# A kernel of attention, a dense block and routed experts: its opening made with one round trip for all key maxima, its routing's scatters spread over three blocks

## The chip, the cores and the metric

The kernel runs on one core of a Trainium2 chip. TensorE (PE) multiplies matrices into PSUM, VectorE (DVE) and ScalarE (ACT) work element by element, GpSimd (POOL) too, and it issues the indirect DMAs; SyncE (SP) issues the other DMAs. Each engine takes its instructions in the order written, so an instruction that waits holds up all that stand behind it on its engine. The metric is device time of one execution in microseconds (us), the median of several runs.

## The reference

Inputs q, k, v have the shape (8, 8, 576, 64): batch, heads, sequence, head size. What is computed, shortened:

```python
q_s = exp(q - max(q, -1)); q_s /= sum(q_s, -1) + 1e-9         # softmax over the head's 64
k_s = exp(k - max(k, 2));  k_s /= sum(k_s, 2) + 1e-9          # softmax over the sequence
kv  = einsum('bhsd,bhse->bhde', k_s, v)
x   = einsum('bhsd,bhde->bhse', q_s, kv)                      # -> 4608 tokens x 512
h   = x @ w_in;  x = (h * clip(h + 3, 0, 6) / 6) @ w_out      # weights stored as float64
e   = argmax(x @ w_gate)                                      # one of 8 experts per token
out = gate * sigmoid(x @ w_output_gate)[e] * (relu(x @ w1[e]) @ w2[e])
```

## The kernel before

The 4608 tokens go through attention and the dense block in 16 groups of 288 (`g`), two for each batch entry `b`. A group's dense block is a loop of 16 blocks (`fb`): four k-steps of `h_mm` (x by a 128-wide slice of w_in, into the PSUM tile `hps`), `h_ev` (ACT's ReLU and DVE's product), and `x2_mm` three blocks later (into four PSUM tiles `acc`). Between these stand the attention of the next group (`att_steps`) and the routing of the group before (`route1` to `route4`). After the groups come tiles of 256 tokens for the experts, each with a gather of its tokens, 8 steps of `h2_mm` and of `y_mm`, and a scatter of its rows. All orders are written out by hand: the text of the program is the order on each engine.

The opening is what stands ahead of block 0 of group 0. Eight DMAs bring k and v of batch entry 0 in four pairs of heads (`hp`, 96 partitions x 768 numbers each), two bring q for group 0 (`a`). For each pair `k_max` reduces six rows to one (DVE), `k_max_tr` transposes it (PE, into `kmps`), `k_max_diag` takes the maximum along the row and puts it on a diagonal (DVE, `mc` and `dg`), `k_max_row` multiplies by ones so that each partition holds the maxima (PE, `kmrow`). That is one round trip between DVE and PE for each pair, four in all, with the rest of the attention between them: `k_sub` (DVE), `k_exp` (ACT), `v_pad` (ACT copies v beside a column of ones), `kv_mm` (PE), `kv_ev` (DVE makes the reciprocal, ACT scales into `kvbd`), `q_a`, `q_exp`, `q_b` (softmax of q), `q_tr` (PE transposes, ACT copies to `qT`), `x0_mm` (PE, ACT copies to `xhi`). `pe_warm` issues matmuls whose result nobody reads.

The weights w_in and w_out come as float64. `dec_act` (L186, L188, ACT) and `dec_vec` (L192, L194, DVE) turn a tile of them into float32 in place; in group 0, `decode_step` does so for the next tiles, between the blocks. In groups 1 and 2, `split` (L200 on ACT, L202 on DVE or POOL) makes a high and a low part of each weight tile for the later groups. Its result goes into a buffer of a pool of 33 (`wsl`), so ACT's cast may have to wait until the tile that sat there has had its last reader.

`route4` of the group before stands in block 11 of each group from 1 on. It ends with three indirect DMAs on POOL (L530), which scatter 96 entries each into the table `tbl` in DRAM. They write one tensor, so the second waits until the first has landed, and the third for the second. Behind them in POOL's queue stand that block's `gl` (L407, low part of the activations) and, in group 2, its half of `split` (L202).

Of the kernel before, what the change touches and what calls it, by code (L numbers as in the profile page):

```python
# [8 lines left out]
F32 = mybir.dt.float32  # L9
# [11 lines left out]
def kernel(  # L21
# [227 lines left out]
    def v_pad(b, hp):  # L249
        t = big([PR, R, 2 * D + 1], F32, "io", 7, "vt")  # L250
        nc.gpsimd.memset(t[:, :, 2 * D:], 1.0)
        nc.scalar.copy(t[:, :, 0:2 * D].rearrange("p r (h d) -> p r h d", h=2), vt[b, hp].rearrange("p h r d -> p r h d"))
        vt[b, hp] = t

    def load_q(g, a):
        b, hf = divmod(g, 2)
        src = lambda h: q[b, 4 * a + h].rearrange("(p r) d -> p r d", r=R)[:, hf * RH:(hf + 1) * RH, :]
        if g < 2:
            t = wsl.tile([PR, 4, RH, D], F32, tag="w", name="qraw")
            nc.sync.dma_start(  # L260
                out=t.rearrange("p h r d -> p h (r d)"),
                in_=q[b, 4 * a:4 * a + 4].rearrange("h (p r) d -> p h (r d)", r=R)[:, :, hf * RH * D:(hf + 1) * RH * D])
            qt[g, a] = t.rearrange("p h r d -> p r h d")
            return
# [58 lines left out]
    def kv_ev(b, hp):  # L323
        ps = kvps.pop((b, hp))
        rs = sb.tile([128, 1], F32, tag="rs", name="rs")
        nc.vector.tensor_scalar(out=rs, in0=ps[:, 2 * D:2 * D + 1], scalar1=1e-9, scalar2=None, op0=ALU.add)
        nc.vector.reciprocal(out=rs, in_=rs)
        for h in range(2):
            a = slice(h * D, (h + 1) * D)
            nc.scalar.activation(out=kvbd[a, hp, a], in_=ps[a, a], func=ACTF.Copy, scale=rs[a])  # L330

    def q_a(g, a):
        t = qt[g, a]
# [5 lines left out]
        eng.tensor_tensor(out=qt[g, a], in0=t, in1=m.unsqueeze(3).to_broadcast([PR, RH, 4, D]), op=ALU.subtract)  # L339

    def q_exp(g, a):
        t = qt[g, a].rearrange("p r h d -> p (r h d)")
        nc.scalar.activation(out=t, in_=t, func=ACTF.Exp)

    def q_b(g, a):
        t = qt[g, a]
        m = sb.tile([PR, RH, 4], F32, tag="qs", name="qs")
        nc.vector.tensor_reduce(out=m, in_=t, axis=AX.X, op=ALU.add)
        nc.vector.tensor_scalar(out=m, in0=m, scalar1=1e-9, scalar2=None, op0=ALU.add)
        nc.vector.reciprocal(out=m, in_=m)  # L350
        eng = nc.gpsimd if g < 2 else nc.vector
        eng.tensor_tensor(out=t, in0=t, in1=m.unsqueeze(3).to_broadcast([PR, RH, 4, D]), op=ALU.mult)

    qT = {}

    def q_tr(g, hp):
        t = qt[g, hp // 2]
        ps = pat.tile([128, 512], F32, tag="a", name="qtps")
        for r in range(RH):
            c = (hp % 2) * 2  # L360
            nc.tensor.transpose(ps[:, r * PR:(r + 1) * PR], t[:, r, c:c + 2, :].rearrange("p h d -> p (h d)"), ident[0:PR, 0:PR])
        s = big([128, G], F32, "qT", 1, "qT")
# [7 lines left out]
    def x0_mm(g, hp):  # L370
        if hp == 0:
            xhi[g] = big([128, KD, G], F32R if g else F32, "xh", 2, "xhi")
            if g:
                xlo[g] = big([128, KD, G], F32R, "xl", 2, "xlo")
        ps = pat.tile([128, 512], F32, tag="a", name="x0ps")
# [133 lines left out]
    def route4(g):  # L509
# [358 lines left out]
    with tc.manual_schedule():  # L868
        constants()
        route_constants()  # L870
        fill_constants()
        load_k(0, 0)
        load_q(0, 0)
        load_k(0, 1)
        load_v(0, 0)
        load_k(0, 2)
        load_q(0, 1)
        load_k(0, 3)
        load_v(0, 1)
# [6 lines left out]
        pe_warm(10)  # L886
        k_max(0, 0)
        k_max_tr(0, 0)
        q_a(0, 0)
        q_exp(0, 0)  # L890
        k_max_diag(0, 0)
        k_max_row(0, 0)
        k_max(0, 1)
        k_max_tr(0, 1)
        k_sub(0, 0)
        k_exp(0, 0)
        v_pad(0, 0)
        k_max_diag(0, 1)
        k_max_row(0, 1)
        q_b(0, 0)  # L900
        k_max(0, 2)
        k_sub(0, 1)
        k_max_tr(0, 2)
        k_exp(0, 1)
        v_pad(0, 1)
        kv_mm(0, 0)
        k_max_diag(0, 2)
        k_max_row(0, 2)
        kv_ev(0, 0)
        q_a(0, 1)  # L910
        k_max(0, 3)
        k_sub(0, 2)
        q_tr(0, 0)
        k_max_tr(0, 3)
        kv_mm(0, 1)
        k_exp(0, 2)
        v_pad(0, 2)
        q_exp(0, 1)
        k_max_diag(0, 3)
        k_max_row(0, 3)  # L920
        kv_ev(0, 1)
        k_sub(0, 3)
        x0_mm(0, 0)
        q_tr(0, 1)
# [12 lines left out]
        dec_vec(1)
        x0_mm(0, 2)
        q_tr(0, 3)
        x0_mm(0, 3)  # L940
        dec_act(2)
        dec_act(3)
        for g in range(NG):
            st = att_steps(g + 1)
            for fb in range(NF):
# [29 lines left out]
                if g > 0:  # L975
# [164 lines left out]
```

## Time and profile before

| | |
|---|---|
| median of 3 runs | 1468.23 us (1467.95 to 1469.39) |
| the profiled execution's own time | 1460.46 us |
| its span | 1458.7 us |
| PE busy | 1408.2 us, 97% |
| DVE, ACT, POOL busy | 59%, 46%, 33% |
| mean granted clock of TensorE | 0.986 of full speed |

A row of the timeline gives the start from the span's beginning, the duration, engine, line, operation, the tile written and the tile read, and in brackets the idle time of the engine before it with what ended it. A granted clock of 1.00 is TensorE's level of 2.4 GHz, 0.50 that of 1.2 GHz. PE's busy time comes from modelled ends, so a PE that is always busy may still run at half its clock.

### The profile page before, as it was taken

How to read it: one execution, taken by the hardware profiler on the slowest of the kernel's cores; microseconds unless marked ns; L12 is line 12 of the kernel's file. 1: busy time of each engine (PE TensorE's matmuls, PEld its weight loads, DVE VectorE, ACT ScalarE, POOL GpSimd, SP SyncE). 2: the span in 40 equal slices, each digit the busy share in tenths (PEclk: the TensorE clock that was granted, in tenths of full speed). 3: DMA queues.
4: the chain of work that ended last, by engine and by line, in shares of the span. 5: the costliest groups of instructions: out<-in, count | busy, mean ns of one | idle time of the engine just before them, and what ended most of it. 6: DMA issues, size and time to landing. Idle time of an engine off the chain costs nothing. (4 is left out here: it accounts for less than half of the span.)

```text
span 1458.7 us, 27464 instructions
## 1 busy us (share of the span) xinstructions
PE 1408.2 (97%) x9668; PEld 1322.5 (91%) x9668; DVE 860.7 (59%) x2151; ACT 670.4 (46%) x1479; POOL 486.8 (33%) x544
## 2 busy tenths in 40 slices
PE   6999998999999999999999999999999999999997
PEld 5788998999999999999999999999888898998996
DVE  6976364545634735545554473637868676767743
ACT  5854353433433433343343343334645565655643
POOL 1113363222222222222322222344444545455431
PEclk7999999999999999999999999999999999999999
DMA  9912021121220202212122020034767677877774
GB/s 292 322 39 58 21 51 27 44 50 25 56 53 18 53 14 58 52 24 58 26 50 50 17 58 17 2 99 137 235 195 217 210 227 224 246 221 245 231 253 147
DMA packets 195749, 161.17 MB, mean 110 GB/s; under 512 B 116828, under 2 KB 147793, under 8 KB 195602
## 3 DMA queue, kind: packets, MB, share of 16 engines
q1 hardware_dynamic: 186114, 139.51, 33.5%
q0 software_dynamic: 9488, 19.82, 4.2%
q8 instruction: 78, 1.28, 0.4%
q14 instruction: 69, 0.57, 0.1%
HBM read 139.03 MB, written 20.49 MB: 109 GB/s over the span
## 5 line engine op out<-in xcount | busy, mean ns | idle before, releaser
L390 PE MATMUL hps<-xhi,w 128*128 128x288 f32 x1920 | 427.9, 298 | 0.0
L418 PE MATMUL acc<-gh,w 128*128 128x288 f32 x1800 | 410.7, 306 | 0.0
L407 POOL TENSOR_TENSOR gl<-r,gh 128x288 fp32r<-128x288 f32 x225 | 182.0, 810 | 540.9 <-ACT gh L406 510.0
L390 PEld LDWEIGHTS hps<-xhi,w 128*128 128x128 f32 x1920 | 321.4, 188 | 1.5
L418 PEld LDWEIGHTS acc<-gh,w 128*128 128x128 f32 x1800 | 301.7, 189 | 3.4
L390 PE MATMUL hps<-xlo,w 128*128 128x288 f32 x960 | 283.2, 295 | 0.0
L400 DVE SCALAR_TENSOR_TENSOR r<-r,hps 128x288 f32<-128x288 f32 x225 | 101.4, 451 | 306.8 <-ACT r L399 298.9
L418 PE MATMUL acc<-gl,w 128*128 128x288 f32 x900 | 265.7, 295 | 0.0
L399 ACT ACTIVATE r<-hps,half 128x288 f32<-128x288 f32 x225 | 112.6, 500 | 263.2 <-PE hps L390 258.8
L821 PE MATMUL h2ps<-x2h,wb 128*128 128x256 f32 x1088 | 216.9, 282 | 1.6 <-issue 1.3
L772 POOL DMA_INDIRECT gx<-x2d,idx x148 | 163.8, 1106 | 140.0 <-issue 126.2
L737 DVE TENSOR_TENSOR wb<-rawb,wb 128x512 fp32r<-128x512 f32 x296 | 191.6, 688 | 13.7 <-ACT wb L736 6.1
L839 PE MATMUL y<-wb,hh 128*128 128x512 f32 x592 | 190.6, 403 | 0.8 <-issue 0.8
L821 PEld LDWEIGHTS h2ps<-x2h,wb 128*128 128x128 f32 x1088 | 176.6, 189 | 9.3 <-issue 2.4
L390 PEld LDWEIGHTS hps<-xlo,w 128*128 128x128 f32 x960 | 181.0, 189 | 0.8
L418 PEld LDWEIGHTS acc<-gl,w 128*128 128x128 f32 x900 | 170.8, 190 | 2.9
L736 ACT CAST wb<-rawb 128x512 fp32r<-128x512 f32 x296 | 168.3, 619 | 2.6 <-DMA rawb<-in_moe_w_dram 2.3
L406 ACT CAST gh<-r 128x288 fp32r<-128x288 f32 x225 | 97.4, 433 | 140.4 <-DVE r L400 139.9
L821 PE MATMUL h2ps<-x2l,wb 128*128 128x256 f32 x544 | 152.8, 281 | 8.0 <-DVE x2l L802 6.9
L825 ACT ACTIVATE hh<-h2ps 128x256 fp32r<-128x256 f32 (+1 forms) x160 | 58.9, 369 | 176.1 <-PE h2ps L821 95.7
L826 DVE SCALAR_TENSOR_TENSOR hl<-h2ps,hh 128x256 fp32r<-128x256 f32 (+1 forms) x160 | 62.9, 395 | 116.1 <-issue 58.0
L839 PE MATMUL y<-wb,hl 128*128 128x512 f32 x296 | 117.9, 398 | 0.3 <-issue 0.3
(201 smaller groups left out, 1810.5 us busy)
## 6 DMA issues: line engine op xcount, KB each, us to landing
rawb<-in_moe_w_dram SPq DMA_DIRECT2D x296, 256.0 KB
x2d<-xrow SPq DMA_DIRECT2D x60, 144.0 KB
raw<-in_moe_w_in_dram SPq DMA_DIRECT2D x16, 512.0 KB
raw<-in_moe_w_out_dram SPq DMA_DIRECT2D x16, 512.0 KB
qt<-in_q_dram SPq DMA_DIRECT2D x112, 72.0 KB
kt<-in_k_dram SPq DMA_DIRECT2D x56, 144.0 KB
vt<-in_v_dram SPq DMA_DIRECT2D x56, 144.0 KB
w1h<-in_moe_w_dram SPq DMA_DIRECT2D x24, 256.0 KB
```

Source lines behind the costliest of these rows:

```text
L390: nc.tensor.matmul(ps[:, 0:G], weight("in", fb, part, kk), x[:, kk, :], start=(n == 0), stop=(n == len(parts) * KD - 1))
L399: nc.scalar.activation(out=r, in_=ps[:, 0:G], func=ACTF.Relu, bias=half, scale=1.0 / 6.0)
L400: nc.vector.scalar_tensor_tensor(out=r, in0=r, scalar=1.0, in1=ps[:, 0:G], op0=ALU.min, op1=ALU.mult)
L406: nc.scalar.copy(gh, r)
L407: nc.gpsimd.tensor_tensor(out=gl, in0=r, in1=gh.bitcast(F32), op=ALU.subtract)
L418: nc.tensor.matmul(acc[g][eb][:, 0:G], weight("out", fb, part, eb), x, start=(fb == 0 and n == 0), stop=(fb == NF - 1 and n == len(parts) ...
L736: nc.scalar.copy(w[:, 0, :], raw)
L737: nc.vector.tensor_tensor(out=w[:, 1, :], in0=raw, in1=w[:, 0, :].bitcast(F32), op=ALU.subtract)
L772: nc.gpsimd.indirect_dma_start(out=st["gx"][:, kk, :], out_offset=None, in_=x2q, in_offset=bass.IndirectOffsetOnAxis(ap=st["idx"][:, kk:kk ...
L821: nc.tensor.matmul(ps[:, 0:m], w[:, wl, c], x[:, kk, 0:m], start=(kk == 0 and n == 0), stop=(kk == KD - 1 and n == 2))
L826: nc.vector.scalar_tensor_tensor(out=hl[:, 0:m], in0=ps[:, 0:m], scalar=0.0, in1=hh[:, 0:m].bitcast(F32), op0=ALU.max, op1=ALU.subtract)
L839: nc.tensor.matmul(st["y"][t2], hx[:, c], w[:, wl, :], start=(fb == 0 and n == 0), stop=(fb == NF2 - 1 and n == 2))
```

## The change

Two things, in the diff below. First, the opening. SP issues the four k tiles first, then q and v. `first_max` takes the maximum of a pair's six rows with three DVE operations in place of one reduction, and all four transposes go into one PSUM tile. `first_row` then makes one reduction, one diagonal of 512 columns, and one matmul of 512 columns. `pe_warm` stands between these steps: 8, four times 2, 4, and 6. The subtraction for q moves to POOL for both halves and works in place, as does `k_sub`; the copy of v for the last pair moves to POOL; `kv_ev` scales the first two pairs on DVE. `kv_mm` of the four pairs stands ahead of all `q_tr` and `x0_mm`; `dec_act(1)` stands behind the last `x0_mm`. Second, `route4` no longer issues its scatters; a new function `scatter` issues one in each of blocks 11, 12 and 13 (for the last group: in steps 3, 4 and 5 of expert tile 4).

```diff
+    def first_max(hp):
+        if hp == 0:
+            first["st"] = big([128, 2, 512], F32, "xh", 2, "first")
+            first["tr"] = pat.tile([128, 512], F32, tag="a", name="kmps0")
+        t = kt[0, hp]
+        m3 = big([PR, 3, 2, D], F32, "xs", 3, "km3")
+        m = first["st"][0:PR, 0, hp * 128:(hp + 1) * 128]
+        mv = m.rearrange("p (h d) -> p h d", h=2)
+        nc.vector.tensor_tensor(out=m3, in0=t[:, 0:3], in1=t[:, 3:6], op=ALU.max)
+        nc.vector.tensor_tensor(out=mv, in0=m3[:, 0], in1=m3[:, 1], op=ALU.max)
+        nc.vector.tensor_tensor(out=mv, in0=mv, in1=m3[:, 2], op=ALU.max)
+        nc.tensor.transpose(first["tr"][:, hp * PR:(hp + 1) * PR], m, ident[0:PR, 0:PR])
+    def first_row():
...
+        nc.vector.tensor_reduce(out=mc, in_=first.pop("tr")[:, 0:4 * PR].rearrange("p (i s) -> p i s", s=PR),
+                                axis=AX.X, op=ALU.max)
+        dg = first["st"][:, 1, :]
+        nc.vector.tensor_tensor(out=dg.rearrange("p (i d) -> p i d", i=4),
...
+        pe_warm(4)
+        ps = pat.tile([128, 512], F32, tag="a", name="kmrow0")
+        nc.tensor.matmul(ps[0:PR, :], onesf, dg, start=True, stop=True)
...
+    def first_qmax(a):
+        m = sb.tile([PR, RH, 4], F32, tag="qm", name="qm")
+        nc.vector.tensor_reduce(out=m, in_=qt[0, a], axis=AX.X, op=ALU.max)
+        nc.gpsimd.tensor_tensor(out=qt[0, a], in0=qt[0, a], in1=m.unsqueeze(3).to_broadcast([PR, RH, 4, D]),
+                                op=ALU.subtract)
...
-        for r in range(RH):
-            nc.gpsimd.indirect_dma_start(
-                out=tv, out_offset=bass.IndirectOffsetOnAxis(ap=posi[:, r:r + 1], axis=0),
-                in_=ent[:, r, :], in_offset=None)
+        rt[g] = tv, posi, ent
+
+    def scatter(g, r):
+        tv, posi, ent = rt[g]
+        nc.gpsimd.indirect_dma_start(
+            out=tv, out_offset=bass.IndirectOffsetOnAxis(ap=posi[:, r:r + 1], axis=0),
+            in_=ent[:, r, :], in_offset=None)
...
                     if fb == 11:
                         route4(g - 1)
+                    if 11 <= fb < 11 + RH:
+                        scatter(g - 1, fb - 11)
```

The opening's order on DVE, from the first key tile on, before: one pair's maximum (L275), maximum along the row (L288), diagonal (L292) and subtraction (L306), and then the next pair's.

```order
L275 TENSOR_REDUCE km<-kraw 96x128
L335 TENSOR_REDUCE qm<-qraw 96x12
L339 TENSOR_TENSOR qt<-qraw,qm 96x768
L288 TENSOR_REDUCE mc<-kmps 128x1
L292 TENSOR_SCALAR dg<-ident,mc 128x128
L275 TENSOR_REDUCE km<-kraw 96x128
L306 TENSOR_TENSOR kt<-kraw,kmrow 96x768
L288 TENSOR_REDUCE mc<-kmps 128x1
L292 TENSOR_SCALAR dg<-ident,mc 128x128
L348 TENSOR_REDUCE qs<-qt 96x12
```

The same engine and place now, from the last pair's maximum on (three operations, L281 to L283; `first` holds the maxima and later the diagonals).

```order
L281 TENSOR_TENSOR km_228<-kraw 96x384
L282 TENSOR_TENSOR first<-km_228 96x128
L283 TENSOR_TENSOR first<-first,km_228 96x128
L288 TENSOR_REDUCE mc_236<-kmps_203 128x4
L291 TENSOR_TENSOR first<-ident,mc_236 128x512
L302 TENSOR_REDUCE qm<-qraw 96x12
L340 TENSOR_TENSOR kraw<-kraw,kmrow_244 96x6x2x64 x2
L302 TENSOR_REDUCE qm<-qraw 96x12
L340 TENSOR_TENSOR kraw<-kraw,kmrow_244 96x6x2x64 x2
L390 TENSOR_REDUCE qs<-qraw 96x12
```

The four subtractions now stand behind the last pair's arrival, and nothing but q's maxima stands between them.

POOL in group 2 around the scatters of group 1, before (`w` is the low half that `split` makes, `gl` that of the activations).

```order
L202 TENSOR_TENSOR w<-raw,w 128x512
L530 DMA tbl<-ent,posi 43264x4 x3
L407 TENSOR_TENSOR gl<-r,gh 128x288
L202 TENSOR_TENSOR w<-raw,w 128x512
L407 TENSOR_TENSOR gl<-r,gh 128x288
L202 TENSOR_TENSOR w<-raw,w 128x512
```

The same place now.

```order
L577 DMA tbl<-ent,posi 43264x4
L451 TENSOR_TENSOR gl<-r,gh 128x288
L202 TENSOR_TENSOR w<-raw,w 128x512
L577 DMA tbl<-ent,posi 43264x4
L451 TENSOR_TENSOR gl<-r,gh 128x288
L202 TENSOR_TENSOR w<-raw,w 128x512
L577 DMA tbl<-ent,posi 43264x4
L451 TENSOR_TENSOR gl<-r,gh 128x288
```

One block's `gl` and `w` now stand between each scatter and the next.

## Rows read from the trace of the kernel before

**Rows 1.** The page: busy time of PE, and a group of DVE operations.

```profile
PE 1408.2 (97%) x9668; PEld 1322.5 (91%) x9668; DVE 860.7 (59%) x2151; ACT 670.4 (46%) x1479; POOL 486.8 (33%) x544
...
L737 DVE TENSOR_TENSOR wb<-rawb,wb 128x512 fp32r<-128x512 f32 x296 | 191.6, 688 | 13.7 <-ACT wb L736 6.1
```

**Rows 2.** Waits of PE over the whole run: waiter, awaited, total us, times, longest.

```profile
PE x0ps L376 <- ACT qT L363: 7.0, 4, 4.5
```

**Rows 3.** Windows of the opening: busy us by engine, then granted clock, DMA share, GB/s.

```profile
0.00:5.00 5.00, 3.45 (x16) 3.45 (x17) 2.65 (x22) 1.28 (x1) 1.75 (x13) 1.00 0.63 156
5.00:10.00 5.00, 1.88 (x10) 1.21 (x9) 4.85 (x7) 0.84 (x1) 0.00 (x0) 0.87 1.09 252
25.00:30.00 5.00, 5.00 (x26) 4.71 (x26) 1.92 (x5) 3.86 (x8) 1.47 (x1) 0.58 1.06 323
30.00:35.00 5.00, 2.89 (x16) 2.13 (x15) 1.71 (x4) 3.60 (x9) 0.00 (x0) 1.00 1.07 375
```

**Rows 4.** Timeline of the opening and of the first blocks, PE, DVE and ACT.

```profile
1.55 4.29 PE L220 MATMUL warm<-ident 128*128 128x128 f32 x20 [1.55 <-POOL ident L94]
4.20 1.47 DVE L275 TENSOR_REDUCE km<-kraw 96x128 f32<-96x768 f32 x1 [1.09 <-DMA kraw<-in_k_dram]
34.28 0.40 ACT L377 COPY xhi<-x0ps 128x288 f32<-128x288 f32 x1 [0.84 <-PE x0ps L376]
39.57 0.49 ACT L399 ACTIVATE g<-hps,half 128x288 f32<-128x288 f32 x1
40.60 2.22 PE L390 MATMUL hps<-xhi,raw 128*128 128x288 f32 x8 [2.47 <-DVE g L400]
43.62 2.22 PE L390 MATMUL hps<-xhi,raw 128*128 128x288 f32 x8 [0.81 <-DVE g L400]
```

**Rows 5.** Groups of instructions from 0 to 34 us: busy us, mean ns, idle before.

```profile
L319 PE MATMUL kvps<-vt,kt 96*128 96x129 f32 x48 | 10.6, 405 | 0.0
L306 DVE TENSOR_TENSOR kt<-kraw,kmrow 96x768 f32<-96x768 f32 x4 | 3.8, 942 | 0.1
L311 ACT ACTIVATE kt<-kt 96x768 f32<-96x768 f32 x4 | 3.4, 843 | 6.3 <-DVE kt L306 6.3
L352 POOL TENSOR_TENSOR qt<-qt,qs 96x768 f32<-96x768 f32 x2 | 2.9, 1469 | 11.8 <-DVE qs L350 11.8
L348 DVE TENSOR_REDUCE qs<-qt 96x12 f32<-96x768 f32 x2 | 1.9, 942 | 0.0
L363 ACT COPY qT<-qtps 128x288 f32<-128x288 f32 x4 | 1.6, 400 | 1.8 <-PE qtps L361 1.8
L330 ACT ACTIVATE kvbd<-kvps,rs 64x64 f32<-64x64 f32 x8 | 2.5, 306 | 1.7 <-PE kmrow L298 1.7
L288 DVE TENSOR_REDUCE mc<-kmps 128x1 f32<-128x96 f32 x4 | 1.0, 246 | 0.0
L186 ACT ACTIVATE raw<-raw,floorb 128x512 int32<-128x512 uint16 x2 | 1.5, 757 | 0.0
L188 ACT ACTIVATE raw<-raw 128x512 f32<-128x512 f32 x2 | 1.3, 644 | 0.0
```

**Rows 6.** Timeline of PE, one pair of keys later in the run.

```profile
119.50 1.50 PE L319 MATMUL kvps<-vt,kt 96*128 96x129 f32 x12
```

**Rows 7.** Timeline of DVE, an operation of the decode, while POOL runs one.

```profile
51.12 1.85 DVE L194 SCALAR_TENSOR_TENSOR raw<-raw 128x512 int32<-128x512 int32 x1
```

**Rows 8.** Timeline of group 2 around the scatters: POOL, ACT, PE.

```profile
217.52 0.91 POOL L530 DMA_INDIRECT tbl<-ent,posi  x1 [2.06 <-DMA tbl<-ent,posi]
222.03 1.29 POOL L202 TENSOR_TENSOR w<-raw,w 128x512 fp32r<-128x512 f32 x1
223.35 0.65 ACT L200 CAST w<-raw 128x512 fp32r<-128x512 f32 x1 [5.40 <-POOL w L202]
224.35 1.33 PE L376 MATMUL x0ps<-qT,kvbd 128*128 128x288 f32 x2 [4.48 <-ACT qT L363]
```

**Rows 9.** Window of group 2 behind the stall.

```profile
224.00:227.00 3.00, 2.65 (x9) 2.37 (x10) 0.84 (x2) 1.99 (x6) 2.57 (x4) 0.50 0.00 0
```

More of the change, by code (lines that the diff above doesn't have):

```diff
@@ L251, in v_pad @@
         nc.gpsimd.memset(t[:, :, 2 * D:], 1.0)
-        nc.scalar.copy(t[:, :, 0:2 * D].rearrange("p r (h d) -> p r h d", h=2), vt[b, hp].rearrange("p h r d -> p r h d"))
+        cp = nc.gpsimd.tensor_copy if hp == 3 else nc.scalar.copy
+        cp(t[:, :, 0:2 * D].rearrange("p r (h d) -> p r h d", h=2), vt[b, hp].rearrange("p h r d -> p r h d"))
         vt[b, hp] = t
@@ L309, in k_exp @@
     def k_exp(b, hp):
+        if b == 0:
+            t = big([PR, R, 2, D], F32, "io", 7, "kt")
+            nc.scalar.activation(out=t, in_=kt[b, hp], func=ACTF.Exp)
+            kt[b, hp] = t
+            return
         t = kt[b, hp].rearrange("p r h d -> p (r h d)")
@@ L329, in kv_ev @@
             a = slice(h * D, (h + 1) * D)
-            nc.scalar.activation(out=kvbd[a, hp, a], in_=ps[a, a], func=ACTF.Copy, scale=rs[a])
+            if b == 0 and hp < 2:
+                nc.vector.tensor_scalar(out=kvbd[a, hp, a], in0=ps[a, a], scalar1=rs[a], scalar2=None, op0=ALU.mult)
+            else:
+                nc.scalar.activation(out=kvbd[a, hp, a], in_=ps[a, a], func=ACTF.Copy, scale=rs[a])
     def q_a(g, a):
@@ L341, in q_exp @@
     def q_exp(g, a):
-        t = qt[g, a].rearrange("p r h d -> p (r h d)")
+        t = qt[g, a] if g == 0 else qt[g, a].rearrange("p r h d -> p (r h d)")
         nc.scalar.activation(out=t, in_=t, func=ACTF.Exp)
@@ L361, in q_tr @@
             nc.tensor.transpose(ps[:, r * PR:(r + 1) * PR], t[:, r, c:c + 2, :].rearrange("p h d -> p (h d)"), ident[0:PR, 0:PR])
-        s = big([128, G], F32, "qT", 1, "qT")
+        s = big([128, G], F32, "r", 2, "qT") if g == 0 and hp % 2 else big([128, G], F32, "qT", 1, "qT")
         nc.scalar.copy(s, ps[:, 0:G])
@@ L374, in x0_mm @@
                 xlo[g] = big([128, KD, G], F32R, "xl", 2, "xlo")
-        ps = pat.tile([128, 512], F32, tag="a", name="x0ps")
+        ps = pat.tile([128, 512], F32, tag="a", name="x0ps") if g else ph.tile([128, 512], F32, tag="h", name="x0ps0")
         nc.tensor.matmul(ps[:, 0:G], kvbd[:, hp, :], qT.pop((g, hp)), start=True, stop=True)
@@ L871 @@
         fill_constants()
-        load_k(0, 0)
+        for hp in range(4):
+            load_k(0, hp)
         load_q(0, 0)
-        load_k(0, 1)
         load_v(0, 0)
-        load_k(0, 2)
+        load_v(0, 1)
         load_q(0, 1)
-        load_k(0, 3)
-        load_v(0, 1)
         load_v(0, 2)
@@ L885 @@
         load_w_raw(14)
[L886 to L894, printed above, removed]
+        pe_warm(8)
+        for hp in range(4):
+            first_max(hp)
+            pe_warm(2)
+        first_row()
+        pe_warm(6)
+        first_qmax(0)
+        v_pad(0, 0)
+        v_pad(0, 1)
         k_sub(0, 0)
         k_exp(0, 0)
-        v_pad(0, 0)
-        k_max_diag(0, 1)
-        k_max_row(0, 1)
-        q_b(0, 0)
[L901 to L917, printed above, removed]
-        q_exp(0, 1)
[L919 to L924, printed above, removed]
+        kv_mm(0, 0)
+        k_sub(0, 1)
+        q_exp(0, 0)
+        k_exp(0, 1)
+        kv_mm(0, 1)
+        first_qmax(1)
+        k_sub(0, 2)
+        v_pad(0, 2)
+        k_exp(0, 2)
+        kv_mm(0, 2)
+        v_pad(0, 3)
+        k_sub(0, 3)
+        q_b(0, 0)
+        q_exp(0, 1)
         k_exp(0, 3)
-        v_pad(0, 3)
-        kv_mm(0, 2)
+        kv_mm(0, 3)
         q_b(0, 1)
         dec_act(0)
+        kv_ev(0, 0)
+        kv_ev(0, 1)
+        q_tr(0, 0)
+        q_tr(0, 1)
+        x0_mm(0, 0)
         x0_mm(0, 1)
         kv_ev(0, 2)
+        q_tr(0, 2)
+        kv_ev(0, 3)
+        q_tr(0, 3)
+        x0_mm(0, 2)
+        x0_mm(0, 3)
         dec_vec(0)
-        kv_mm(0, 3)
-        q_tr(0, 2)
         dec_act(1)
-        kv_ev(0, 3)
         dec_vec(1)
-        x0_mm(0, 2)
-        q_tr(0, 3)
-        x0_mm(0, 3)
         dec_act(2)
@@ L1027, in tile_steps @@
                     route4(NG - 1)
+                if t == 4 and 3 <= fb < 3 + RH:
+                    scatter(NG - 1, fb - 3)
                 if (t, fb) == (0, 1) or (t in (2, 3, 4) and fb % 2):
```

12 lines of the change are left out of this document (9 added, 3 removed).

## Prediction

> **What bounds the kernel now.** I read the page's busy times first: PE is busy for 1408.2 of 1458.7 us [rows 1], so 50 us at most are to be had where PE stands still, and whatever shortens another engine's work is worth nothing unless PE waits for it. The second view is the opening in windows: from 5 to 15 us PE is busy less than half the time, and the granted clock falls to 0.50 and is back at 1.00 only in the window from 30 us on [rows 3]. The third is the timeline of the opening, where the reader should find four points: the first key tile arrives at 4.20, the last part of x is copied out at 34.28 to 34.68, block 2 of the dense part starts at 40.60 after PE idled 2.47 us for DVE's `g`, block 3 at 43.62 [rows 4]. From block 3 on PE has no such gap in group 0 as these; so what the opening ends earlier, up to block 3, the whole run ends earlier. The fourth is the list of PE's waits over the run: 7.0 us in four waits for ACT's `qT`, the longest 4.5 us [rows 2]. That long one is in group 2, right where the scatters of group 1 stand.
>
> **The scatters.** In group 2 POOL issues the second scatter at 217.52 after 2.06 us of waiting for the first to land; the low half of a weight tile, which stands behind all three, starts at 222.03 [rows 8]. ACT's next cast takes a buffer that this operation must have read first: it starts at 223.35, after 5.40 us of idling for POOL; `qT` follows it on ACT, and PE, which needs `qT`, idles 4.48 us until 224.35 [rows 8]. Then the granted clock is at 0.50 from 224 to 227 [rows 9], so some 2.8 us of work take twice as long as they need: 1.4 us more. Sum 5.9 us. With one scatter in each block POOL does this after the first one ends (217.52 - 2.06 = 215.46): `gl` 0.80 (an estimate from the low half of a tile, 1.29 for 512 columns [rows 8], by 288), then the low half 1.29, done at 217.6. The cast that waited can start at 217.95, when ACT began to idle (223.35 - 5.40). So the wait goes, with 0.4 us to spare, and `qT` has another 0.9 us before PE wants it at 219.87 (224.35 - 4.48). The second scatter comes after 217.6, when the first has landed, the third a block later: no new wait. Ends: 0 if something else holds the buffer, 5.9 if all goes; I take 5.9. In the other groups no cast stands in ACT's way, and only three other waits for `qT` are on the list, 2.5 us together; I count nothing there. For the last group's scatters nothing stands between them on POOL; also nothing.
>
> **The opening, up to the last key maximum.** A pair of keys is 295 KB, and the queue moves 252 GB/s [rows 3], 1.17 us a pair. The first is there at 4.20 [rows 4], so the fourth at 7.7 at the earliest; I take 8.5, between that and the 9.4 that a rate lower by a third would give. A two-input DVE operation takes 0.69 us for 512 numbers [rows 1] and 0.94 for 768 [rows 5], so 0.55 for 384 and 0.29 for 128: 1.2 us for a pair's three with their gaps, in place of the 1.47 of one reduction [rows 4]. Last pair done at 9.7; transpose 0.35; the reduction of 4 x 96 numbers 0.54 (0.25 for 96 [rows 5], 0.94 for 768); the diagonal 0.69. `dg` stands at 11.3. PE meanwhile has six warm matmuls, 12 passes, between the last transpose and the matmul by ones. The 20 passes of the first 4.29 us took 0.21 each [rows 4]; 12 passes later in the run 1.50 us, 0.11 to 0.125 each [rows 6]. The clock column says 1.00 for both, so the first were at the lower level in spite of it. At the lower level the six end at 12.6 and hold the matmul by ones back by 1.3 us, at the upper at 11.4. That matmul's two passes of 512 columns take 1.7 or 0.9 us. I call its end K: 12.4 at the upper level, 14.5 at the lower.
>
> **From K to x.** DVE: four subtractions, one reduction for q's maximum, one for q's sum, six of 0.94 that overlap slightly, K+5.3. ACT: seven of 0.84 (four exponentials of keys, two of q, one copy), K+6.4, and PE's last `kv_mm` 1.5 us later, K+7.9 [rows 5 and 6]. POOL: q's second subtraction to K+4.4 and the copy of v, which no row shows on POOL; the bounds are 0 and 1.5 us (two inputs of that size take 1.47 [rows 5]), I take 1.5: K+5.9. Now DVE and POOL meet. While POOL ran a two-input operation, a DVE operation that takes 0.69 us for that size took 1.85 [rows 7 and 1]. So I let the small additions behind q's two sums wait for POOL: q's first product on POOL K+6.3 to 7.8, second K+8.2 to 9.7, DVE's `kv_ev` for two pairs K+8.2 to 9.75. Then PE's `x0_mm` 0 and 1, and ACT in a row: copy of x 0 and 1 to K+10.9, then `kvbd` 0.63, `qT` 0.40, `kvbd` 0.63, `qT` 0.40, x 0.40 [rows 5], K+13.3; `x0_mm` 3 and its copy, K+14.0. That is 26.4 or 28.5 for the end of x; I take the middle, 27.4, against 34.68.
>
> A rule of the Trainium skill speaks against moving work to POOL: GPSIMD Engine Reference, § Engine selection, says to keep elementwise work on VectorE, since GpSimd is about half as fast with two inputs and near line rate with one. The rows show 1.47 against 0.94 us, a factor of 1.6 and not 2. By the rule's half the subtractions would take 1.9 us and the products too, and the opening would end 1.2 us later (three of these stand one behind the other); by its line rate for the copy, 0.7 us earlier.
>
> **What is late next.** `dec_act(1)` now stands behind x. Before, four `dec_act` (0.76 + 0.64 each, overlapping [rows 5]; 4.9 us from 34.68 to 39.57) separated x from the first `h_ev`; now five do, 6.1 us. With `h_ev` 0.5 and DVE's 0.5, block 2 starts 7.1 us behind x, not 5.9: 34.5 in place of 40.60. Block 3 follows 3.0 us later as before, since two `dec_act` and one `h_ev` stand between them either way. Weights: they move at 323 to 375 GB/s [rows 3], 512 KB in 1.5 us, two tiles in 3 us; a block takes 3.9 us of PE, so six us earlier they are still ahead. Gain of the opening 6.1 us, from 5.0 (K = 14.5) to 7.2 (K = 12.4).
>
> **The sum.** 5.9 + 6.1 = 12.0 us off the profiled execution's own 1460.46 us: 1448.5. The median of the runs shown is 7.8 us above that execution; I carry the difference unchanged: 1468.2 - 12.0 = 1456.2 us.
>
> **Rivals.** (1) PE's clock stays at 0.50 through the whole opening. For it: the clock fell after PE idled in the window from 5 to 10 us and took until about 29 us to return although PE was almost always busy from 20 us on [rows 3]. Against it: the warm matmuls now fill the gaps. Price: K = 14.5, six more warm matmuls 2.6 us, four `kv_mm` of 12 passes at 0.22 us 10.6 us, then the transposes, `x0_mm` and ACT's row as above but with PE's parts doubled: x ends near 35.1, block 2 at 42.2, 1.6 us later than before. With the scatters: 1463.9 us. (2) The stall in group 2 stays, because the buffer's last reader is another or a scatter still stands ahead of it when it matters: the change does half of what it says. Only the opening counts: 1462.1 us. The spare 0.4 us speaks for it, ACT's bracket that names POOL's operation against it. (3) Both: about no change, 1469.8. (4) The other side: slower. A scatter in blocks 12 and 13 holds POOL until the one before has landed, 2.06 us in the row, ahead of that block's `gl`. A block lasts some 3.6 us; wait, issue 0.91 and `gl` 0.80 are 3.8 where the landing comes no earlier than its issue's block. Once POOL lags more than the three blocks by which `gl` runs ahead of `x2_mm`, PE waits in each of 14 groups; at 1.3 us each that is 18 us more, 1474 us. Against it: the wait runs from the earlier scatter's issue, a block ago, and POOL is busy 33%.
>
> **How the numbers follow.** Forecast 0.72; its own range is 1453 to 1459.5: 1.1 us for K either way, 0.7 for POOL's copy, about 1.5 for a gap of PE that costs its clock or doesn't. Rival 1 0.09, rival 2 0.09, rival 3 0.05, rival 4 0.05. A measurement of this kernel can tell 0.2%, 2.9 us, from no change; so faster is 0.72 + 0.09 + 0.09 = 0.90, the same 0.05, slower 0.05. The range that holds 8 in 10 takes in rivals 1 and 2: 1452 to 1464.
>
> **What would show it.** Right: x's last copy near 27 us; block 2 near 34.5; no idle of ACT for `w` in group 2 and no half clock there; `mc` reduced once. Wrong: a granted clock of 0.50 from 9 to 25 us, PE's `kmrow` late behind warm matmuls by more than 2 us, a `qT` wait of several us still in group 2, or a new wait of PE for `gl` in blocks 12 to 15. The forecast falls if block 3 of group 0 doesn't start at least 4 us earlier.

## The result, and the profile after

Five runs of the changed kernel, beside five of the kernel before: median 1452.7 us (1445.0 to 1458.73) against 1467.95 (1465.1 to 1469.39); the ratio is 0.9896, 95% interval 0.9874 to 0.9918. So it is faster, by 15.2 us (1.0%) where 12.0 were forecast. That lies in the wider range, 1452 to 1464, and 0.3 us below the forecast's own, which began at 1453. The profiled execution took 1445.0 us, its span is 1443.3 (before: 1460.46 and 1458.7).

First the views that answer to those of before. The page of the changed kernel:

```profile
span 1443.3 us, 27517 instructions
...
PE 1407.1 (97%) x9694; PEld 1322.0 (92%) x9694; DVE 858.8 (60%) x2156; ACT 668.3 (46%) x1474; POOL 493.9 (34%) x546
```

PE is busy for as long as before to 1.1 us [rows 1]; what went is time in which it stood still. The opening in windows, and one window of group 2 (from, to, length, busy time of PE, PEld, DVE, ACT, POOL, granted clock, DMA share, GB/s):

```profile
0.00:5.00 5.00, 3.44 (x16) 3.45 (x16) 2.63 (x23) 1.28 (x1) 1.71 (x12) 1.00 0.61 149
5.00:10.00 5.00, 3.75 (x22) 2.96 (x22) 3.92 (x12) 0.00 (x0) 0.00 (x0) 1.00 1.09 251
25.00:30.00 5.00, 3.43 (x13) 2.52 (x14) 2.15 (x4) 4.43 (x9) 0.00 (x0) 1.00 1.05 336
30.00:35.00 5.00, 2.94 (x11) 1.93 (x10) 3.76 (x7) 5.00 (x10) 0.00 (x0) 0.92 1.07 379
219.00:222.00 3.00, 3.00 (x25) 3.00 (x24) 0.00 (x0) 0.44 (x1) 0.12 (x1) 1.00 0.00 0
```

Between the windows of [rows 3], the trace of before has:

```profile
20.00:25.00 5.00, 4.85 (x22) 4.02 (x21) 2.86 (x9) 3.55 (x7) 0.10 (x1) 0.50 1.08 318
```

Against these: from 5 to 10 us PE has twice the work (the warm matmuls), and the clock stays at 1.00 to 30 us, where it was 0.50 from 20 to 25 and 0.58 from 25 to 30. In the opening it falls once, after PE idled 2 us ahead of block 2. The last window answers to [rows 9]: PE works through it at the upper level. The timeline of the same opening, then of POOL and ACT in group 2 (start, length, engine, line, operation, idle before and what ended it):

```profile
9.57 1.53 PE L220 MATMUL warm<-ident 128*128 128x128 f32 x12
9.77 0.56 DVE L288 TENSOR_REDUCE mc<-kmps 128x4 f32<-128x384 f32 x1 [0.39 <-PE kmps L284]
11.19 1.10 PE L296 MATMUL kmrow<-first,onesf 128*96 128x512 f32 x2
14.29 5.98 PE L358 MATMUL kvps<-vt,kt 96*128 96x129 f32 x48 [0.67 <-ACT kt L346]
16.57 0.82 POOL L253 COPY vt<-vraw 96x768 f32<-96x768 f32 x1
17.62 0.17 DVE L391 TENSOR_SCALAR qs<-qs 96x12 f32<-96x12 f32 x1
18.22 1.47 POOL L396 TENSOR_TENSOR qt<-qraw,qs 96x768 f32<-96x768 f32 x1 [0.83 <-DVE qs L392]
18.90 0.82 DVE L391 TENSOR_SCALAR qs<-qs 96x12 f32<-96x12 f32 x1
26.00 0.40 ACT L421 COPY xhi<-x0ps 128x288 f32<-128x288 f32 x1 [0.54 <-PE x0ps L420]
29.26 2.22 PE L434 MATMUL hps<-xhi,raw 128*128 128x288 f32 x8 [1.36 <-DVE raw L194]
32.51 0.49 ACT L443 ACTIVATE g<-hps,half 128x288 f32<-128x288 f32 x1
33.54 4.63 PE L434 MATMUL hps<-xhi,raw 128*128 128x288 f32 x11 [2.06 <-DVE g L444]
...
207.62 0.93 POOL L577 DMA_INDIRECT tbl<-ent,posi  x1 [0.85 <-DVE ent L571]
209.33 1.31 POOL L202 TENSOR_TENSOR w<-raw,w 128x512 fp32r<-128x512 f32 x1
210.81 0.91 POOL L577 DMA_INDIRECT tbl<-ent,posi  x1 [0.17 <-issue]
214.10 0.92 POOL L577 DMA_INDIRECT tbl<-ent,posi  x1 [0.29 <-DMA tbl<-ent,posi]
...
210.98 0.65 ACT L200 CAST w<-raw 128x512 fp32r<-128x512 f32 x1
```

One `mc`; x complete at 26.40 in place of 34.68, block 2 at 33.54 in place of 40.60 [rows 4]. In group 2 the low half ends at 210.64 and ACT's cast starts at 210.98 without a wait, where it idled 5.40 us [rows 8]; the later scatters wait 0.17 and 0.29 us. PE's waits over the run (waiter, awaited, total us, times, longest):

```profile
PE x0ps L420 <- ACT qT L407: 1.7, 3, 0.9
PE hps L434 <- DVE g L444: 2.1, 1, 2.1
PE h2ps L868 <- DVE x2l L849: 3.8, 6, 1.5
```

The wait for `qT` of 4.5 us [rows 2] is gone.

**Where the time went.** I set the start of each PE matmul in one trace against the start of the same matmul in the trace of before; the difference is how far the kernel is ahead there ("by position" below). Read at four places: at the first accumulation of group 0 (behind block 3), at 200 us, at 300 (group 2 over), at 990 (the last dense group). The next column is the time from the first expert matmul to PE's last; then the timed median and the median of the kernel before on the same chip. Lines of one group of runs stand together; each of the four later groups had a chip of its own.

```
                        block 3   200    300    990   experts    median   before
before                                                 443.9    1467.95
changed                   6.5     6.9   12.8   10.8    440.8    1452.70  1467.95

a0 changed again          6.3     6.8   12.7   10.7    430.5    1435.30  1446.43
e1 scatters only         -0.2    -0.1    6.0    5.9    430.7    1440.09  1446.43
e2 opening only           7.6     7.6    8.0    6.0    429.9    1440.84  1446.43
e3 no warm matmuls        4.6     5.1   11.0    9.0    429.2    1437.97  1446.43

b0 before again           1.1     1.7    0.9    0.8    448.4    1463.83  1459.40
e4 h_ev first             7.1     7.1   12.9   10.9    440.6    1445.24  1459.40
e6 low half on DVE        0.4     0.5    6.5    6.5    448.0    1454.46  1459.40
e5 dec_act(1) early too   7.0     7.0   12.9   10.9    442.1    1442.69  1459.40

a1 changed, third time    6.8     7.3   13.1   11.2    453.0    1454.49  1467.13
e7 order of need         10.3     9.4   15.2   13.2    449.5    1453.04  1467.13
e8 one trip, old engines  6.0     6.0   11.7    9.7    446.8    1459.18  1467.13

e9 order and pad         11.7    10.9   16.9   16.7    428.9    1427.20  1446.92
```

Two gains, 6.9 us ahead of group 2 and 5.9 in it; then a slow loss of 2.0 between 300 and 990 us; then the expert phase, which changes by more than the whole gain from chip to chip. The last two were not foreseen. The "before" column carries that last point best: the unchanged kernel's own median runs from 1446.4 to 1468.0 us over five groups of runs. And "before again" shows that the old opening varies too: it is 1.1 to 1.7 us ahead of its own first trace before group 2, with a granted clock of 0.70 from 20 to 25 us where the first had 0.50; against it, the new opening gains 5.2 us at 200 us.

### The profile page after: what moved, and what is told of

The parts are those of the page before. It is cut to its first block, busy times and chain, and to the rows that moved or that the text cites. A ratio compares the mean times of both kernels' runs of the same rounds, so it can differ in the third digit from the quotient of the medians.

```text
span 1443.3 us, 27517 instructions
## 1 busy us (share of the span) xinstructions
PE 1407.1 (97%) x9694; PEld 1322.0 (92%) x9694; DVE 858.8 (60%) x2156; ACT 668.3 (46%) x1474; POOL 493.9 (34%) x546
```

## The experiments

**a0 and a1: the changed kernel twice more, unaltered.**

> The changed kernel once more, unaltered. By position of the same matmul against the kernel before, the first profile stood 6.9 us ahead from block 6 of group 0 on, 12.8 us from the fourth quarter of group 2 on, 10.8 at the end of the dense part, 18 near 1120 us of the expert phase and 13.9 at the last matmul. Theory A (opening and group 2 are the change, the rest is how one execution differs from another): again 6.9 and 12.8 within 0.5 us, but another figure from 1000 us on. Rival (the expert phase is changed too): again 18 near 1120 us and the same stalls as in the first profile at the same places.

Measured: ratio 0.993 (0.9915 to 0.9945), 11.1 us. The first 300 us repeat to 0.2 us, the expert phase takes 430.5 us and not 440.8: theory A. The 2.0 us between 300 and 990 us come again (12.7 to 10.7), so they are no accident of one execution.

> The changed kernel a third time, unaltered, for the total and as the partner of the other kernels of this group. Theory A (the part of the change that is there in every execution is that of the opening and of group 2): block 3 of group 0 at 36.5 to 37.5 us, 12.8 us ahead of the old profile after group 2, total 10 to 12 us under the kernel before; anything beyond 12 has come in the expert phase. Rival (the change is worth 15 us wherever it runs): total 14 to 17 us under the kernel before.

Measured: ratio 0.9916 (0.9891 to 0.9941), 12.6 us; 13.1 ahead at 300 us, but 453.0 us in the expert phase. PE's waits from 1000 to 1440 us, of a0 (the whole list) and of a1 (the longest three):

```profile
PE h2ps L868 <- DVE x2l L849: 2.5, 1, 2.5
```

```profile
PE h2ps L868 <- DVE x2l L849: 5.7, 5, 3.8
PE y L886 <- issue: 5.0, 9, 1.2
PE lgps L489 <- issue: 3.6, 1, 3.6
```

One program, two chips: on one PE waits once in the expert phase, on the other over and over, in part for nothing that the profile shows. What differs between the chips is not settled.

**e1 and e2: each half alone.** e1 is the kernel before with the `scatter` of the diff; e2 is the changed kernel with

```
                     if fb == 11:
                         route4(g - 1)
-                    if 11 <= fb < 11 + RH:
-                        scatter(g - 1, fb - 11)
+                        for r in range(RH):
+                            scatter(g - 1, r)
```

> The kernel before with the three scatters in three blocks, its opening untouched. Theory: no stall of PE for qT near 220 us and no half clock there; 0 ahead until group 2, 5.9 us ahead from there, so about 1462 us where the kernel before takes 1468 (ratio 0.996). Rival (the shorter opening removes the stall by shifting group 2's weights, and not the scatters): the 4.5 us wait for qT in group 2 stays, ratio 1.000. Rival (POOL is held by scatters in blocks 12 and 13): new waits for gl, ratio over 1.002.

> The changed kernel with the three scatters of a group one behind the other again, in block 11. Theory: 6.9 us ahead of the kernel before from block 6 of group 0 on, no more after group 2, and a wait for qT of 4 to 5 us in group 2 with the clock at 0.50 after it; about 1461 us where the kernel before takes 1468 (ratio 0.995). Rival (the stall went with the opening): 12.8 us ahead after group 2, as in the changed kernel, ratio 0.990.

Measured: e1 0.9955 (0.9939 to 0.9971), 6.3 us; e2 0.9967 (0.9954 to 0.998), 5.6 us. Together 11.9, both at once 11.1: the halves add up. e1 jumps from 0.1 behind to 6.0 ahead in group 2 and keeps it to a tenth; all other groups give nothing, and both of its rivals are out. e2 has the old stall at its new place:

```profile
213.68 1.29 POOL L202 TENSOR_TENSOR w<-raw,w 128x512 fp32r<-128x512 f32 x1
215.00 0.65 ACT L200 CAST w<-raw 128x512 fp32r<-128x512 f32 x1 [4.67 <-POOL w L202]
216.00 0.75 PE L420 MATMUL x0ps<-qT,kvbd 128*128 128x288 f32 x2 [3.75 <-ACT qT L407]
```

These three rows repeat [rows 8] 8.35 us earlier, with waits 0.7 us shorter. e2's opening came out 0.7 us better than expected. At block 2 it is 0.6 us ahead of the changed kernel's profile (32.98 against 33.54), since its last key maximum came earlier; and its clock did not fall there, after the same 2 us of idling. And e2 also loses 2.0 us from 300 to 990 us, e1 nothing: the slow loss came with the opening.

**e3: without the warm matmuls.** Only `pe_warm(8)` stays.

```
             first_max(hp)
-            pe_warm(2)
         first_row()
-        pe_warm(6)
...
-        pe_warm(4)
         ps = pat.tile([128, 512], F32, tag="a", name="kmrow0")
```

> The changed kernel without the warm matmuls between the maxima, ahead of kmrow and behind it (8 + 4 + 6 of them); the 8 at the start stay. Theory (the warm matmuls hold the clock up, and PE's pace counts in the opening): granted clock 0.50 from about 9 us until near 29 us, the four kv_mm 2.6 us each in place of 1.5, x complete at 31 to 33 us in place of 26.4, block 3 at 41 to 44 us in place of 36.9, total 4 to 7 us more than the changed kernel. Rival (ACT, DVE and POOL set the opening whatever the clock is): x within 1 us of 26.4 and the total within 1 us of the changed kernel, or up to 1 us less since kmrow does not wait behind warm matmuls.

Measured: ratio 0.9951 (0.9933 to 0.9969), 2.7 us more than a0; block 3 1.7 us later. Windows and timeline of e3:

```profile
5.00:10.00 5.00, 1.67 (x6) 0.66 (x5) 3.89 (x11) 0.00 (x0) 0.00 (x0) 0.88 1.09 254
10.00:15.00 5.00, 2.02 (x2) 0.39 (x2) 3.63 (x6) 2.59 (x4) 1.56 (x3) 0.50 1.10 251
15.00:20.00 5.00, 4.94 (x27) 4.97 (x28) 4.90 (x8) 5.00 (x8) 3.32 (x5) 0.59 1.10 350
20.00:25.00 5.00, 4.76 (x40) 4.18 (x38) 4.28 (x16) 2.04 (x6) 1.93 (x2) 1.00 1.09 320
```

```profile
11.03 2.02 PE L295 MATMUL kmrow<-first,onesf 128*96 128x512 f32 x2 [1.45 <-DVE first L291]
15.06 7.52 PE L357 MATMUL kvps<-vt,kt 96*128 96x129 f32 x48 [2.01 <-ACT kt L345]
27.86 0.40 ACT L420 COPY xhi<-x0ps 128x288 f32<-128x288 f32 x1 [0.54 <-PE x0ps L419]
```

The clock falls, as the theory has it: PE idles for 3.3 of the 5 us from 5 to 10 us and is granted 0.50 behind that. But it is back at 1.00 by 20 us, where before it took until about 29 us [rows 3], so only part of the `kv_mm` runs at the lower level: 7.52 us in place of 5.98. x is complete at 28.26, 1.9 us later. Theory and rival were both off; the warm matmuls are worth 1.7 us and not 4 to 7.

**b0: the kernel before once more.**

> The kernel before, unaltered, profiled again. The kernels with one half of the change each (scatters alone, opening alone) both passed the expert phase some 13 us faster than the profile of before that the prediction was read from. Theory A (that profile's expert phase was one slow execution, the change does nothing there): by position this profile is within 0.5 us of the old one up to 1000 us, with the same wait for qT in group 2, and 11 to 15 us ahead of it at the last matmul. Rival (either half shortens the expert phase): within 3 us of the old profile at the last matmul.

Measured: one run, 1463.83 us; up to 990 us within 2 us of the old trace, with the stall in group 2; 448.4 us in the expert phase, and 3.7 us behind the old trace at the last matmul. Theory A falls: that profile was no slow accident. The rival's 3 us are missed by 0.7. With a0 and a1 beside it, it is the chip that decides most: 430 us on the first, 440 to 448 on this one, 447 to 453 on the third. On b0's chip both kernels with the old opening stand at 448 and both with the new at 440.6 and 442.1, on a0's chip old and new differ by 0.2. Whether the new opening helps there on some chips stays open; the first pair (443.9 and 440.8) has room for 3 us of it.

**e6: why the scatters cost anything.**

```
-        eng = nc.vector if kind == "in" and f < 3 else nc.gpsimd
+        eng = nc.vector if (kind == "in" and f < 3) or (kind == "out" and f in (12, 13)) else nc.gpsimd
```

> The kernel before with its scatters together, but the low halves of the weight tiles out 12 and out 13 (group 2) computed on DVE and not on POOL. Theory (the scatters cost PE time only because the low half behind them keeps a buffer from ACT's cast): ACT's 5.4 us wait for w and PE's 4.5 us wait for qT in group 2 go, the clock stays at 1.00, 5 to 6 us ahead of the kernel before from the end of group 2 on, ratio about 0.996, as with the scatters spread. Rival (gl behind the scatters holds PE as well): PE waits 2 us or more for gl in blocks 12 to 15 of group 2, less than 3.5 us gained.

Measured: 0.9964 (0.9946 to 0.9981), 6.0 us gained in group 2 by position, with the scatters as they were. In e6:

```profile
219.16 0.91 POOL L530 DMA_INDIRECT tbl<-ent,posi  x1 [1.90 <-DMA tbl<-ent,posi]
218.03 0.69 DVE L202 TENSOR_TENSOR w<-raw,w 128x512 fp32r<-128x512 f32 x1 [1.06 <-ACT w L200]
217.34 0.66 ACT L200 CAST w<-raw 128x512 fp32r<-128x512 f32 x1
220.94 0.50 ACT L399 ACTIVATE r<-hps,half 128x288 f32<-128x288 f32 x1 [2.65 <-POOL gl L407]
```

The scatter still waits 1.90 us for the one before, and ACT waits 2.65 us for the `gl` behind the scatters; PE has no wait for either, since ACT's cast finds its buffer read. So the 5.9 us were not the scatters' own time but one low half that stood behind them, as the prediction said; spreading them is one of two cures.

**e4, e5 and e7: the row of `dec_act` behind x.** e4 puts `h_ev(0, 0)` ahead of `decode_step(1)` and leaves it out in its old place:

```
+                if g == 0 and fb == 0:
+                    h_ev(0, 0)
```

> The changed kernel with h_ev of block 0 put ahead of decode_step(1), so that three dec_act stand between x and the first h_ev in place of five. Theory (the row of dec_act on ACT sets block 2): h_ev at about 30.2 in place of 32.5, block 2 at 31.4 (behind block 1 on PE) in place of 33.5, no 2 us idle of PE ahead of it and no 0.50 clock at 34 us; block 3 at 33.5 to 34.5 in place of 36.9; total 2 to 3 us less than the changed kernel. Rival (raw tiles, DVE's dec_vec or the weights' arrival hold block 2 or 3): block 3 at 36 to 37 as before and total within 0.7 us.

Measured: 0.9908 (0.9887 to 0.993). The blocks of e4:

```profile
32.15 2.22 PE L434 MATMUL hps<-xhi,raw 128*128 128x288 f32 x8 [0.95 <-DVE raw L194]
36.50 2.22 PE L434 MATMUL hps<-xhi,raw 128*128 128x288 f32 x8 [2.14 <-DVE g L444]
```

Block 2 comes 1.4 us earlier than in the changed kernel, block 3 only 0.4: the wait moved one block on, since four `dec_act` now stand ahead of the next `h_ev`. So the rival's numbers hold (block 3 at 36.5, 0.1 us gained by position at 300 us), but what holds block 3 is still `g` behind a row of `dec_act`; only block 2 waits for DVE's `raw`, 0.95 us. The clock stayed up. e5 also moves `dec_act(1)` ahead and passes over one `xhi` buffer:

```
         dec_act(0)
+        dec_act(1)
         kv_ev(0, 0)
...
+            big([128, 2, 512], F32, "xh", 2, "skip")
             first["st"] = big([128, 2, 512], F32, "xh", 2, "first")
```

> The changed kernel with h_ev of block 0 ahead of decode_step(1), with dec_act(1) ahead of the kv_ev and q_tr copies on ACT, and with one buffer of the two of xhi passed over, so that xhi[0] lies where it lay in the kernel before. Theory: two dec_act between x and the first h_ev; x up to 0.6 us later, block 1 right behind block 0, block 3 at 32.5 to 33.5, another 0.7 to 1.2 us ahead of the kernel with h_ev first alone. On the buffer: the kernels with the new opening lose 1.7 to 1.9 us against the kernel before between 300 and 1000 us, a little in every matmul; theory (xhi's place): this kernel loses less than 0.4 us there; rival (another buffer or not a buffer at all): again 1.6 to 1.9.

Measured: 0.9883 (0.9864 to 0.9903). Block 3 at 36.60, no better than e4, and the slow loss unchanged: both theories missed. One part of the miss is the clock: in e5 it stood at 0.50 from 8.8 to 12.2 us, the 12 warm passes ahead of `kmrow` took 2.66 us in place of 1.53, and `kmrow` ended at 13.33 in place of e4's 12.01. Counted from there, block 3 comes 1.2 us earlier than in e4; PE still waits 2.1 us for `g` ahead of it. e7 moves `dec_act(1)` as e5 does, orders all of the first decodings by need, and turns the rings of q, k, v and x's rows on by further unused tiles like e5's (five of `io`, two of `xs`). A ring is the set of buffers that the tiles of one tag take in turn:

```
+    def first_decode(fb):
+        if fb == 0:
+            dec_vec(2)
+            h_ev(0, 0)
+            dec_vec(3)
+            dec_act(4)
+        elif fb == 1:
+            h_ev(0, 1)
+            dec_vec(4)
+            dec_act(5)
+            dec_vec(5)
+        elif fb == 2:
+            h_ev(0, 2)
+            dec_act(6)
+            dec_act(7)
+        else:
+            decode_step(fb)
...
-                    decode_step(fb + 1)
+                    first_decode(fb)
```

> The changed kernel with the first decodings in the order of need: dec_act(1) ahead of the kv_ev copies, and in blocks 0 to 2 of group 0 h_ev ahead of the dec_act that no block needs yet (one dec_act in block 0, one in block 1, two in block 2). With h_ev first in block 0 alone, the wait of 2 us moved from block 2 to block 3, behind four dec_act. Theory (that row alone is what holds blocks 2 and 3): block 2 at 31 to 31.5, block 3 at 33 to 34 in place of 36.9, total 3 to 4 us less than the changed kernel. Rival (the wait only moves on, to block 4 or 5): at block 6 no more than 1 us ahead of the changed kernel. On the slow loss of 1.9 us between 300 and 1000 us, which keeping xhi's place did not remove: here the rings that hold q, k and v and the rows of x are turned back as well; theory (a place in SBUF): under 0.4 us lost there; rival (not a place): 1.6 to 1.9 again.

Measured: 0.9905 (0.9884 to 0.9926), 1.4 us under a1, which these runs can't tell from nothing. In e7:

```profile
12.31 1.46 PE L319 MATMUL kmrow<-first,onesf 128*96 128x512 f32 x2
27.29 8.29 PE L457 MATMUL hps<-xhi,raw 128*128 128x288 f32 x32
35.41 2.10 PE L485 MATMUL acc<-g,raw 128*128 128x288 f32 x8
51.92 0.47 PE L428 MATMUL qtps<-ident,qt 96*128 96x96 f32 x3 [0.47 <-POOL qt L419]
```

Four blocks in a row without a gap: block 3 ends 3.5 us ahead of a1's, although `kmrow` ends 1.8 us later (13.77 against 11.98: here too the clock stood at 0.50, from 9.8 to 13.2 us, and the 12 warm passes took 2.79 us). Of the 3.5 us, 2.1 last; the rest goes up to 64 us, in part waiting for the next group's `q`. The turned rings did nothing for the slow loss.

**e8: what the regrouping is worth.**

```
-        cp = nc.gpsimd.tensor_copy if hp == 3 else nc.scalar.copy
+        cp = nc.scalar.copy
...
-        nc.gpsimd.tensor_tensor(out=qt[0, a], in0=qt[0, a], in1=m.unsqueeze(3).to_broadcast([PR, RH, 4, D]),
+        (nc.gpsimd if a else nc.vector).tensor_tensor(out=qt[0, a], in0=qt[0, a], in1=m.unsqueeze(3).to_broadcast([PR, RH, 4, D]),
...
-            if b == 0 and hp < 2:
+            if False:
```

> The changed kernel with one round trip for all key pairs and the new order of the queues, but with the work on the engines where it was: the fourth copy of v and both early kv_ev on ACT, the first subtraction of q on DVE. Theory (moving work off ACT and DVE is worth something once PE and the round trips no longer set the opening): x complete 1.5 to 2.5 us later than 26.4, block 3 at 38.4 to 39.4, total 1.5 to 2.5 us more than the changed kernel. Rival (the round trip is all): x within 0.5 us of 26.4 and block 3 at 36.9.

Measured: 0.9945 (0.9923 to 0.9966), 4.7 us above a1 by the medians, 1.4 at 300 us by position. In e8:

```profile
20.65 1.27 ACT L372 ACTIVATE kvbd<-kvps,rs 64x64 f32<-64x64 f32 x4
27.05 0.40 ACT L421 COPY xhi<-x0ps 128x288 f32<-128x288 f32 x1 [0.54 <-PE x0ps L420]
34.59 2.22 PE L434 MATMUL hps<-xhi,raw 128*128 128x288 f32 x8 [2.07 <-DVE g L444]
```

x is complete at 27.45, 1.0 us later than in the changed kernel's first profile and 1.4 later than in a1, whose `kmrow` ends at the same time: under the 1.5 to 2.5 expected and over the rival's 0.5. The 4.7 us by the medians go beyond what the opening shows. So moving work off ACT and DVE is worth some 1.4 us of the 6.9, and the warm matmuls 1.7 (e3). What the one round trip, the maximum by three operations and the new order of the loads are worth each, no run separates.

**e9: the slow loss.** In the programs' allocations `gh`, `gl` and `xhi`, which PE streams in the blocks, begin at multiples of 64 bytes in the kernel before and 32 past one in the changed kernel. e9 is e7 without the turned rings and with

```
+            sb.tile([128, 8], F32, tag="pad", name="pad", bufs=1)
             first["st"] = big([128, 2, 512], F32, "xh", 2, "first")
```

> The first decodings in the order of need, as in the kernel before this one, without the turned rings, and a tile of 32 bytes per partition allocated ahead of the opening's first large one. In the kernel before, gh, gl and xhi (what PE's h_mm and x2_mm stream) begin at addresses in SBUF that divide by 64; in the changed kernel, whose new tiles shift them, at 32 past such an address; the tile of 32 bytes puts them back on 64. Turning the rings, tried before, moved no ring's own beginning. Theory (a begin off 64 costs each of these matmuls some 0.5 ns): the shift against the kernel before stays constant between 300 and 1000 us, under 0.4 us lost in place of 1.9, so about 15 us ahead at 1000 us in place of 13.2; total 1.5 to 2 us less than with the order alone, 13 to 15 us under the kernel before where the expert phase adds nothing. Rival (the loss has nothing to do with addresses): again 1.7 to 2.1 us lost.

Measured: 1427.2 us, 19.7 us under the kernel before; 0.9855 (0.9838 to 0.9871), the best of all. From 300 to 990 us it loses 0.2 us (16.9 to 16.7), as the theory had it, and the pad is what took the loss away. Of the 3.5 us by which e9 is ahead of e7 at 990 us, 1.5 were there by 200 us: `kmrow` ended at 12.34 in e9, without the fall of the clock that e7 had. By position 16.7 us are the dense part's; the other 3 can't be placed, since no trace of the kernel before was taken on that chip.

The reason that the theory gives, a begin off 64, does not come out of the traces. The mean time from one matmul's start to the next one's, from 300 to 985 us (steps over 200 ns left out), by what the two matmuls stream:

```
step            before   changed     e9      (ns)
xhi then xlo     133.8     132.4   133.2
xlo then xhi     132.7     133.9   131.0
xhi then xhi     131.8     132.9   132.8
gh then gl       132.6     131.8   132.3
gl then gh       132.2     134.0   133.0
gh then gh       132.3     133.2   133.4
```

Each is a mean of over 500 steps; the other traces with the old opening agree with "before" within 0.3 ns, those with the new one and no pad with "changed" within 0.2. In e9 `gh` and `xhi` are back on multiples of 64, yet `gh` then `gh` and `xhi` then `xhi` are as slow as without the pad, and `xlo` then `xhi` is faster than in either of the others; `xlo` begins 32 past a multiple of 64 in all three programs. So the total came out as forecast, but not for the reason given, and that is luck: some steps gained what others kept losing. That the buffers' places set the pace is shown; which rule they follow stays open.

## Why the prediction was right, step by step

**The scatters: right in place, mechanism and size.** 5.9 us forecast, 5.9 to 6.1 measured three ways (changed kernel 6.9 to 12.8, e1 alone, e6 by the other cure). The spare time was said to be 0.4 us; the low half ends 0.34 before the cast starts. Rivals 2 and 3 (the stall stays) are out. So is rival 4: the second scatter waits 0.17 us and not 2.06, because its turn comes a block later, and no wait of PE for `gl` appears.

**The opening: 6.1 us forecast, measured 7.1 at block 2, 6.5 behind block 3 and 6.9 from 64 us on.** The term that was mis-sized is K. I took the middle of two clock levels; rival 1 (0.50 throughout) didn't come, the 12 warm passes take 1.53 us, the upper level's pace, and K is 12.3 against 12.4 for that level. That was the luck of this execution: K is 11.7 to 12.4 in seven of the nine profiles that have these instructions up to K, but 13.3 in e5 and 13.8 in e7, where the clock was at 0.50 for 3.4 us. The 14.5 for the lower level took it to last until `kmrow`'s end; in both it ended before that. From K on the chain holds almost to the tenth: x is complete 14.1 us behind K (K + 14.0 was forecast) in all eight of these profiles that leave the work on the engines where the change puts it, early K or late, and block 2 comes at 33.5 (x + 7.1). Of the 7.1 us gained there, 0.6 go at blocks 2 and 3, which run in part at the lower level behind the gap of 2.06 us; 0.5 come back from 61 to 64 us, in part from a wait of PE for `q` that the kernel before has there. Two errors inside it cancel or don't matter: POOL's copy of v took 0.82 us and not the 1.5 assumed, and of DVE's two small additions only the second was held (0.82 against 0.17; it ends at 19.72, POOL's product at 19.69). The Trainium skill, SBUF — State Buffer, § SBUF: two separate sides, says that when a GpSimd operation and a VectorE operation that needs the port pair which both share (in a two-port mode, or with two inputs) meet, the first to start has the pair for its whole instruction. These two ends agree; which mode the addition ran in, no row shows. By the Trainium skill, GPSIMD Engine Reference, § Engine selection, a copy on GpSimd runs near line rate; the trace agrees, 0.82 us where ACT takes 0.83 for a tile of the same size. The second part of its rule, half speed with two inputs, the trace doesn't bear out here: 1.47 us on POOL, 0.94 on DVE.

**What is late next** was named rightly (five `dec_act`, then `g`). Its price at block 3 is 3.5 us in e7 with its late K, 4.9 in e9 (11.7 against a1's 6.8). Not named was a wait of 1.36 us for DVE's `raw` ahead of block 1; it costs nothing in the changed kernel, where block 2 waits for `g` in any case.

**What the sum lacked.** First, a cost of new tiles: they moved the buffers that stand behind them, and the 4469 matmuls of `h_mm` and `x2_mm` between 300 and 990 us lost 2.0 us, which a pad of 32 bytes took away (e9). No row of the profile of before shows such a price. Second, that the expert phase is no constant to carry over: by the first two profiles it gave 3.1 us, and 1.5 more lie behind PE's last matmul, which together make the 15.4 us between the two spans. On another chip it gave 0.2 (a0 against e1). So 12.0 lies near the 11.1 and 12.6 of the later groups, and near the 10.8 that the first pair shows up to the experts. That the first gave 15.2, and so came to the edge of the range, lies in the expert phase and behind it, and no run ties that part to the change. That 12.0 fits the totals as well as it does is in part luck: the 2.0 us lost were not in the sum, nor what the expert phase gave.

## What to carry to other kernels

Ask of a slow step what stands behind it in its engine's queue: here three waiting scatters cost PE nothing themselves, and one cast's buffer behind them cost 5.9 us; either can be moved. When a chain at the start is shortened, look at the row of work that now follows it, and order it by what PE needs next. Compare two traces matmul by matmul, not total by total: a jump shows a stall, a slope shows something in many instructions, such as where their buffers lie. And a pad that takes a loss away does not show why the loss was there: look at the kinds of instruction one by one.

## What the runs showed of the hardware

- Where the streamed buffers lie in SBUF changes the pace of PE's matmuls of 288 columns by up to 3 ns from one start to the next, either way (e9's table). By the sum it cost 2.0 us over 4469 matmuls in the changed kernel, 0.45 ns each on the mean, and 0.2 us with 32 bytes of pad. Beginning on a multiple of 64 alone does not decide it.
- The same idling of about 2 us ahead of block 2 was followed by a granted clock of 0.50 in all three profiles of the changed kernel (0.92, 0.92 and 0.84 in the window from 30 to 35 us) and in e3, and not in e2 or e8; nor in e4 and e5, where 2.14 us of idling stand ahead of block 3. The same opening was at 0.50 ahead of `kmrow` in e5 and e7 and at 1.00 in seven other profiles. The lower level behind a short gap can't be counted on either way.
- Without warm matmuls (e3) the clock fell after PE had been busy 1.67 of 5 us, and was back at 1.00 by 20 us with PE busy 4.94 of the 5 us before.
- The expert phase of one and the same program took 430.5 us on one chip and 453.0 on another.
